# Reordering the prologue and moving attention blocks between matmuls in a fused attention and SwiGLU kernel

## The chip, the cores and the metric

The kernel runs on one core of one Trainium2 chip. The metric is the device time of one execution in microseconds (us), as the median of several executions. One execution of each kernel is also recorded by the hardware profiler; its span, from the first to the last instruction, is about 1.7 us shorter than its time. Engines: PE (tensor engine), ACT (ScalarE), DVE (VectorE), POOL (GpSimd), SP (issues transfers).

## The reference

Windowed attention (768 positions, 4 batches, 8 heads of 64, window 128, 4 sink positions) feeds an RMS-normalized SwiGLU layer:

```python
keep = is_sink | ((rel >= 0) & (rel < window))
scores = np.where(keep, q @ k.T / sqrt(64), -1e9)
x = softmax(scores) @ v                      # to (3072, 512)
xn = x / sqrt(mean(x*x) + 1e-6) * rms_g
g = xn @ w_gate                              # (512, 1536)
out = (g * sigmoid(g) * (xn @ w_val)) @ w_out
```

## The kernel before

Tokens are handled in 24 blocks of 128 (six to a batch). For every block q and k are transposed, scores, exps and masks are made, attention weights multiply v, and the rows are scaled by the RMS: `xr`. Transposing `xr` gives `xnt`, the operand of the gate and value matmuls. Four blocks form a group for the feed-forward part.

The order on PE is written by hand: a list of feed-forward "parts", and a list of attention units with the number of the part that they stand ahead of. In the prologue and in the first half of group 0 the order on DVE is by hand too, and in the prologue also that on ACT.

```python
def run(parts, slots):                # (place, unit): the unit goes ahead of that part
    slots = sorted(slots, key=lambda e: e[0])
    for s, f in enumerate(parts):
        while slots and slots[0][0] <= s:
            slots.pop(0)[1]()
        f()
    while slots:
        slots.pop(0)[1]()

with tc.manual_schedule(engines=MANUAL_ALL):          # the prologue, cut to its end
    ...
    unit_bias(1, 1)
    unit_sp(1, 1)                     # scores of block 1, then two exps on ACT
    unit_rms((0,))
    unit_rms((1,))
    unit_xr(0)                        # on ACT, behind those exps
    unit_xr(1)                        # on DVE
    unit_warm(3)                      # dummy matmuls that nothing uses
    unit_x(0)                         # transposes of xr, copy to xnt
    unit_x(1)
    ...
# group 0, first half: 14 parts, with the units of blocks 2 and 3
byhand = (fa(0, split=True) + fa(2, between=lambda: (unit_rms((2,)), unit_xr(2))) + ...)
first = fa(10) + fq(b3, 0) + fq(b3, 4) + fq(b2, 8) + fq(b3, 8)
# then `first` and the output parts of group 0 (12 parts of four 512-column matmuls),
# with the units of blocks 4 to 9 from the list FIRST (its changed lines are shown below)
```

The matmuls' results go to PSUM, for which the kernel keeps a pool of eight tiles (called banks below), given out in turn; each scores, transposes, gate, value or output tile takes one and holds it until ACT or DVE has read it.

The softmax here doesn't subtract the row's maximum and nothing guards it: scores larger than these inputs give would overflow.

## Time and profile before

| | kernel before |
|---|---|
| time, median (first 3 runs) | 251.42 us (251.39 to 251.6) |
| profiled span, mean granted PE clock | 249.9 us, 1.000 |
| PE busy | 239.6 us, 96% |
| first feed-forward matmul (L649) | 16.59 us |
| first output matmul of group 0 (L734) | 50.69 us |
| first gate matmul of group 1 | 70.69 us |
| ACT busy from 60 to 70 us | 9.4 of 10 us |

A timeline row has the start in us, the duration in us, the engine, the line of the kernel, the operation, its output and inputs, a count, and in brackets the idle time of that engine just before and what ended it. A row of the waits says who waited for whom: total us, times, longest. Since PE is the bound, I follow the three starts of the table and the end of the span: where one of them shifts, the time was lost or won ahead of it. The line of the first stands in the prediction; the other two are:

```profile
50.69 3.62 PE L734 MATMUL po<-wo,hT 128*128 128x512 bf16 x15
...
70.69 1.02 PE L649 MATMUL pg<-xnt,wg 128*128 128x512 bf16 x3
```

Two limits of this trace: it lacks 24 matmul records (1926, where e2 below, with the same matmuls, has 1950), so that some of the 10.3 us of idle time that the prediction counts is not idle: PE's waits of 0.15 us and more between its first and last matmul add up to 4.9 us, not about 6. And it holds no clock records, so its 1.000 is a default; that the clock was full there is read from its matmuls, four of which take 0.86 us.

### The profile page before, as it was taken

Reading aid. Unit: us, or ns where it says so; the run is one execution under the profiler, and the core shown is the slowest. Engines: PE = TensorE matmul, PEld = TensorE weight load, DVE = VectorE, ACT = ScalarE, POOL = GpSimd, SP = SyncE. Lnnn points to the kernel's source line nnn. Section 1 sums busy time; section 2 is a strip of 40 time slices with the busy share of each in tenths; the row PEclk is TensorE's granted clock in tenths of the full one; section 3 lists DMA queues with packets and bytes.
Section 4 is the critical chain, followed back from the end, with each engine's and each line's share of the span. In section 5 each row is a group of like instructions: output and inputs, shape, how many; then the busy total and the mean of one; then the engine's idle time right before and its main releaser. Section 6 shows DMA issues by size and latency. Waiting matters only on the chain.

```text
span 249.9 us, 5124 instructions
## 1 busy us (share of the span) xinstructions
PE 239.6 (96%) x1926; PEld 129.9 (52%) x1950; DVE 162.4 (65%) x379; ACT 142.9 (57%) x328; POOL 104.9 (42%) x141
## 2 busy tenths in 40 slices
PE   8979899999899999999999999999999999999995
PEld 3657598955454444544545444444454444444443
DVE  4857587974748779418778548769248787087800
ACT  3676657759888564874774464774374441233212
POOL 8966776497098998781330200331431000000000
DMA  9999999999939999999100465100530002610012
GB/s 128 142 185 180 190 160 206 164 153 184 133 86 134 141 158 149 138 155 154 29 3 0 91 203 107 24 3 3 132 121 0 0 3 42 169 41 3 1 64 105
DMA packets 104939, 25.51 MB, mean 102 GB/s; under 512 B 94033, under 2 KB 101969, under 8 KB 104914
## 3 DMA queue, kind: packets, MB, share of 16 engines
q0 software_dynamic: 80704, 13.90, 74.2%
q1 hardware_dynamic: 23026, 10.95, 19.7%
q10 hardware_dynamic: 1184, 0.33, 0.6%
q8 instruction: 15, 0.25, 0.4%
q14 instruction: 10, 0.08, 0.1%
HBM read 28.31 MB, written 6.29 MB: 138 GB/s over the span
## 4 chain that ended last, share of the span: by engine, by line
PE 67%; DMA 16%; POOL 8%; issue 5%; ACT 2%; DVE 1%; SPq 0%; POOLq 0%; DVEq 0%
PE po L734 20%; PE pvl L649 19%; PE pg L649 19%; DMA wv<-in_moe_w_val_dram 7%; DMA wo<-in_moe_w_out_dram 5%; DMA v<-in_v_dram 3%; PE pT L428 2%; POOL ks L108 2%; POOL v L121 2%; PE pv L475 2%; PE pv L479 2%; POOL qs L108 1%; POOL wg L140 1%; PE po L716 1%; DMA qkT<-ks 1%
## 5 line engine op out<-in xcount | busy, mean ns | idle before, releaser
L649 PE MATMUL pg<-xnt,wg 128*128 128x512 bf16 (+2 forms) x379 | 73.4, 321 | 1.3 <-ACT xnt L637 0.7
L649 PE MATMUL pvl<-xnt,wv 128*128 128x512 bf16 (+2 forms) x390 | 74.1, 322 | 0.2
L671 DVE SCALAR_TENSOR_TENSOR p<-th,pg 128x512 bf16<-128x512 bf16 x72 | 49.2, 684 | 30.4 <-ACT th L667 30.1
L667 ACT ACTIVATE th<-pg 128x512 bf16<-128x512 f32 x72 | 43.2, 602 | 41.2 <-PE pg L649 39.7
L734 PE MATMUL po<-wo,hT 128*128 128x512 bf16 x267 | 62.4, 379 | 0.5
L681 DVE TENSOR_TENSOR hT<-p,pvl 128x512 bf16<-128x512 bf16 x72 | 49.5, 687 | 8.5 <-PE pvl L649 1.5
L405 POOL TENSOR_SCALAR_AFFINE_SELECT et<-et 128x512 bf16<-128x512 bf16 x28 | 19.3, 696 | 74.4 <-ACT et L437 74.4
L649 PEld LDWEIGHTS <-wv 128*128 128x128 bf16 x392 | 33.8, 98 | 29.0
L649 PEld LDWEIGHTS <-wg 128*128 128x128 bf16 x392 | 32.7, 98 | 27.0 <-issue 1.8
L734 PEld LDWEIGHTS <-hT 128*128 128x128 bf16 x276 | 26.1, 98 | 29.2 <-issue 0.4
L437 ACT ACTIVATE et<-pT 128x512 bf16<-128x512 f32 x72 | 37.7, 613 | 3.8 <-PE pT L428 3.7
L741 ACT ACTIVATE osb<-po 128x512 f32<-128x512 f32 x23 | 13.9, 604 | 32.5 <-PE po L734 25.4
L533 ACT ACTIVATE sq<-x 128x256 bf16<-128x256 bf16 x46 | 19.4, 429 | 11.6 <-DVE x L516 11.2
L121 POOL DMA_DIRECT2D v<-in_v_dram x24 | 21.8, 909 | 4.3 <-DMA wo<-in_moe_w_out_dram 2.3
L108 POOL DMA_DIRECT2D qs<-in_q_dram x23 | 21.1, 916 | 4.6 <-DMA wo<-in_moe_w_out_dram 2.9
L511 DVE RECIPROCAL rden<-pv 128x4 f32<-128x4 f32 x48 | 7.5, 172 | 22.0 <-PE pv L479 21.9
L108 POOL DMA_DIRECT2D ks<-in_k_dram x23 | 20.9, 909 | 1.6 <-DMA wv<-in_moe_w_val_dram 0.5
L516 DVE TENSOR_TENSOR x<-pv,rden 128x256 bf16<-128x256 f32 x48 | 19.6, 422 | 0.9
L596 DVE SCALAR_TENSOR_TENSOR xr<-x,y,gb 128x512 bf16<-128x512 bf16 x22 | 16.5, 798 | 0.3
L410 POOL TENSOR_SCALAR_AFFINE_SELECT et<-et 128x512 bf16<-128x512 bf16 x22 | 14.4, 656 | 0.0
L479 PE MATMUL pv<-v,et 128*128 128x65 bf16 x160 | 12.1, 194 | 1.1 <-DVE et L403 0.9
L428 PE MATMUL pT<-qkT 64*128 64x256 bf16 (+1 forms) x160 | 11.8, 261 | 0.2 <-ACT xnt L637 0.2
(85 smaller groups left out, 194.4 us busy)
## 6 DMA issues: line engine op xcount, KB each, us to landing
out_dram<-osb SPq DMA_DIRECT2D x21, 256.0 KB, 2.4
v<-in_v_dram POOLq DMA_DIRECT2D x24, 128.0 KB, 7.1
qs<-in_q_dram POOLq DMA_DIRECT2D x23, 128.0 KB, 6.8
ks<-in_k_dram POOLq DMA_DIRECT2D x23, 128.0 KB, 6.5
wg<-in_moe_w_gate_dram POOLq DMA_DIRECT2D x6, 256.0 KB, 9.0
wv<-in_moe_w_val_dram POOLq DMA_DIRECT2D x6, 256.0 KB, 8.8
wo<-in_moe_w_out_dram POOLq DMA_DIRECT2D x2, 768.0 KB, 11.2
out_dram<-osb SPq DMA_DIRECT2D x4, 128.0 KB, 2.3
```

Of the source, the lines that this page charges most:

```text
L108: nc.gpsimd.dma_start(out=tl, in_=src[b, :, t * P:(t + 1) * P, :].rearrange("h t d -> t h d"),)
L121: nc.gpsimd.dma_start(out=V16[b][:, t, :, 0:D], in_=v[b, :, t * P:(t + 1) * P, :].rearrange("h t d -> t h d"),)
L405: nc.gpsimd.affine_select(out=ev[:, :, 0, :], in_=ev[:, :, 0, :], compare_op=ALU.is_ge, fill=0.0, base=0, pattern=[[0, x], [1, P]], channe ...
L437: nc.scalar.activation(out=et[:, hi].rearrange("p j n c -> p (j n c)"), in_=banks[u][hi], func=ACT.Exp, scale=inv_sqrt_d,)
L479: nc.tensor.matmul(out=dest, lhsT=E[(g, h, 0)], rhs=V16[b][:, t, h, :], start=(t == 0), stop=True, skip_group_check=True,)
L516: nc.vector.tensor_tensor(out=X16[g][:, heads_of(g, u), :], in0=pvv[:, :, 0:D], in1=RDEN.pop((g, u)).unsqueeze(2).to_broadcast((P, 4, D)), ...
L533: nc.scalar.activation(out=sq, in_=xh, func=ACT.Square, scale=MS_SCALE, accum_out=MS[g - i][:, i, u:u + 1],)
L649: nc.tensor.matmul(out=ps[:, i * w + c0:i * w + c0 + n], lhsT=w_sb[:, kt, ft * P:(ft + 1) * P], rhs=XNT[G][:, kt, cols], start=(kt == 0), ...
L667: nc.scalar.activation(out=st["th"], in_=st["pg"], func=ACT.Tanh, scale=0.5)
L671: nc.vector.scalar_tensor_tensor(out=p1, in0=st["th"], scalar=1.0, in1=st["pg"], op0=ALU.add, op1=ALU.mult,)
L681: LAST[0] = nc.vector.tensor_tensor(out=HT[key][:, i:i + n, cols], in0=p1.rearrange("p (n c) -> p n c", n=n), in1=st["pvl"].rearrange("p ( ...
L734: nc.tensor.matmul(out=st["po"], lhsT=HT[(G, ft // 4)][:, ft % 4, tb * P:(tb + 1) * P], rhs=wo[:, ft, :], start=(ft == 0), stop=(ft == FTN ...
```

## The change

Its intent: a shorter prologue, by putting the work that block 0 and 1 need for `xnt` into one chain, with copies and exps that are only needed later behind it; and fewer waits of PE for masks between 60 and 70 us, by putting more PE work between the steps of attention of blocks 6 to 9.

```diff
 # prologue (cut)
-        unit_bias(0, 0)
-        unit_t1(1, 0)
+        unit_t1(1, 0)
+        unit_bias(0, 0)
         unit_sp(0, 0)
+        unit_t1(1, 1)                       # k of block 1 ahead of the second bias
+        ... both other scores of blocks 0, 1, then the four attention groups ...
+        unit_t1(2, 0, held=True)            # "held": its copy is issued later
+        ...
+        while HELD:
+            HELD.pop(0)()
         unit_bias(1, 1)
-        unit_sp(1, 1)
-        unit_rms((0,))
-        unit_rms((1,))
+        unit_warm(4)
+        unit_sp(1, 1, held=True)            # its exps are issued behind xr
+        unit_rms((0, 1))                    # one group of small operations for two blocks
         unit_xr(0)                          # now on DVE
         unit_xr(1)                          # now on ACT
-        unit_warm(3)
+        unit_bias(2, 0)
+        unit_warm(2)
         unit_x(0)
+        unit_sp(2, 0, held=True)
         unit_x(1)
+        while HELD:
+            HELD.pop(0)()
 # first half of group 0
-            (3, lambda: unit_attend(2)),
-            (6, lambda: unit_t1(3, 0)),
-            (6, lambda: unit_t1(3, 1)),
-            (6, lambda: unit_x(2)),
-            (7, ...),                        # scores of 2 and 3
-            (9, lambda: unit_attend(3)),
-            (10, lambda: (unit_rms((3,)), unit_xr(3))),
+            (2, lambda: unit_attend(2)),
+            (3, lambda: (unit_rms((2,)), unit_xr(2))),
+            (5, lambda: unit_x(2)),
+            (7, lambda: unit_t1(3, 0)),
+            (8, lambda: unit_t1(3, 1)),
+            (8, ...),
+            (10, lambda: unit_attend(3)),
+            (11, lambda: (unit_rms((3,)), unit_xr(3))),
 # FIRST: attention of 6 to 9
-        (14, t(7)), (14, sink(1)), (15, s(6)), (15, t(8)), (16, x(4)), (16, x(5)),
-        (17, attend(6)), (17, s(7)), (18, t(9)), (19, attend(7)), (20, t(10)),
-        (20, sink_scores(1, 2)), (20, s(8)), (21, x(6)), (22, x(7)), (22, t(12)), (22, t(13)),
+        (16, t(7)), (16, sink(1)), (17, s(6)), (18, t(8)), (19, attend(6)), (19, s(7)),
+        (20, x(4)), (20, x(5)), (20, t(9)), (21, attend(7)), (21, sink_scores(1, 2)),
+        (21, s(8)), (22, t(10)), (22, x(6)), (24, x(7)), (24, t(12)), (24, t(13)),
```

The last list is written shorter here than in the code. Apart from these parts, four memsets move to the start, one square of block 0 goes from DVE to ACT, three more dummies are issued, and no work is removed but five small RMS operations.

More of the change, by code (lines that the diff above doesn't have):

```diff
@@ L171 @@
     nc.vector.memset(gb[0:1, 0:P], 1.0)
+    KS0 = []
+    for b in range(B):
+        KS0.append(const.tile([P, HP * KSW], BF16, name=f"ksk{b}"))
+        nc.vector.memset(KS0[b], 0.0)
     magic = const.tile([P, GB], FP32, name="magic")
@@ L256, in transposes, with unit_t1 @@
             )
-    def unit_t1(g, i):
+    HELD = []
+    def unit_t1(g, i, held=False):
         b, t = divmod(g, NT)
@@ L264, in unit_t1, with copy @@
         transposes(ps, (QS, KS_)[i].pop(g), 0)
-        (nc.scalar.copy if g in (2, 3) or g != 1 and i == 0 else nc.vector.tensor_copy)(
-            out=QKT[b][:, i, :, t * P:(t + 1) * P],
-            in_=ps[:, 0:HP * P].rearrange("p (x c) -> p x c", c=P),
-        )
+        def copy():
+            (nc.scalar.copy if g in (2, 3) or g != 1 and i == 0 else nc.vector.tensor_copy)(
+                out=QKT[b][:, i, :, t * P:(t + 1) * P],
+                in_=ps[:, 0:HP * P].rearrange("p (x c) -> p x c", c=P),
+            )
+        HELD.append(copy) if held else copy()
     def by_dma(g):
@@ L292, in unit_sink_k @@
     def unit_sink_k(b):
-        ks = sink.tile([P, HP * KSW], BF16, name="ksk")
-        nc.vector.memset(ks, 0.0)
+        ks = KS0.pop(0)
         ksv = ks.rearrange("p (h c) -> p h c", c=KSW)
@@ L365, in unit_bias, with unit_sp @@
         PTS[(g, n)] = banks
-    def unit_sp(g, n):
+    def unit_sp(g, n, held=False):
         b, t = divmod(g, NT)
@@ L379, in unit_sp, with exps @@
                 )
-        for hi in range(2):
-            et = epool.tile([P, HP, P], BF16, name="etp", bufs=6)
-            nc.scalar.activation(
-                out=et.rearrange("p x c -> p (x c)"), in_=banks[hi],
-                func=ACT.Exp, scale=inv_sqrt_d,
-            )
-            for hp in range(HP):
-                E[(g, 2 * hp + hi, n)] = et[:, hp, :]
+        def exps():
+            for hi in range(2):
+                et = epool.tile([P, HP, P], BF16, name="etp", bufs=6)
+                nc.scalar.activation(
+                    out=et.rearrange("p x c -> p (x c)"), in_=banks[hi],
+                    func=ACT.Exp, scale=inv_sqrt_d,
+                )
+                for hp in range(HP):
+                    E[(g, 2 * hp + hi, n)] = et[:, hp, :]
+        HELD.append(exps) if held else exps()
     def bank(name="pT"):
@@ L526, in unit_sq @@
         sq = xpool.tile([P, 4, D], BF16, name="sq")
-        if g == 0:
+        if (g, u) == (0, 1):
             nc.vector.scalar_tensor_tensor(
@@ L539 @@
     GROUP = {}
-    for gs in [(0,), (1,), (2,), (3,), (4, 5), (6,), (7,)] + [
+    for gs in [(0, 1), (2,), (3,), (4, 5), (6,), (7,)] + [
             tuple(range(g, g + GB)) for g in range(2 * GB, NB, GB)]:
@@ L588, in unit_xr @@
         xr = xpool.tile([P, DM], BF16, name="xr", bufs=4)
-        if g == 0:
+        if g == 1:
             nc.scalar.mul(xr, x16, y)
-        elif g == 1:
+        elif g == 0:
             nc.vector.tensor_scalar(
@@ L784, in unit_attend01 @@
         unit_norm(g, u, PV[(g, u)])
-        unit_sq(g, u)
     with tc.manual_schedule(engines=MANUAL_ALL):
@@ L792 @@
         unit_t1(0, 1)
+        unit_t1(1, 0)
         unit_bias(0, 0)
-        unit_t1(1, 0)
         unit_sp(0, 0)
+        unit_t1(1, 1)
+        unit_bias(0, 1)
+        unit_sp(0, 1)
+        unit_bias(1, 0)
+        unit_sp(1, 0)
         unit_sink_k(0)
-        unit_bias(0, 1)
-        unit_t1(1, 1)
-        unit_sp(0, 1)
         unit_attend01(0, 0)
-        unit_bias(1, 0)
         unit_attend01(0, 1)
-        unit_sp(1, 0)
+        unit_sq(0, 0)
         unit_gt()
         unit_attend01(1, 0)
-        unit_t1(2, 0)
+        unit_sq(1, 0)
+        unit_t1(2, 0, held=True)
         unit_attend01(1, 1)
-        unit_t1(2, 1)
+        unit_sq(1, 1)
+        unit_sq(0, 1)
+        unit_t1(2, 1, held=True)
+        while HELD:
+            HELD.pop(0)()
         unit_bias(1, 1)
-        unit_sp(1, 1)
-        unit_rms((0,))
-        unit_rms((1,))
+        unit_warm(4)
+        unit_sp(1, 1, held=True)
+        unit_rms((0, 1))
         unit_xr(0)
         unit_xr(1)
-        unit_warm(3)
+        unit_bias(2, 0)
+        unit_warm(2)
         unit_x(0)
+        unit_sp(2, 0, held=True)
         unit_x(1)
-        unit_bias(2, 0)
-        unit_sp(2, 0)
+        while HELD:
+            HELD.pop(0)()
     h0 = slice(0, GN // 2)
@@ L828, in fq @@
         return parts_f(0, tuple(range(ft, ft + 4)), cols)
-    byhand = (fa(0, split=True) + fa(2, between=lambda: (unit_rms((2,)), unit_xr(2)))
-              + fa(4) + fq(b2, 0) + fa(6) + fq(b2, 4) + fa(8))
+    byhand = (fa(0, split=True) + fa(2) + fa(4) + fq(b2, 0) + fa(6) + fq(b2, 4) + fa(8))
     first = fa(10) + fq(b3, 0) + fq(b3, 4) + fq(b2, 8) + fq(b3, 8)
@@ L837 @@
             (2, lambda: unit_gb()),
-            (3, lambda: unit_attend(2)),
-            (6, lambda: unit_t1(3, 0)),
-            (6, lambda: unit_t1(3, 1)),
-            (6, lambda: unit_x(2)),
-            (7, lambda: unit_sink_scores(0, 3, 1)),
-            (7, lambda: unit_bias(2, 1)),
-            (7, lambda: unit_sp(2, 1)),
-            (7, lambda: unit_bias(3, 0)),
-            (7, lambda: unit_sp(3, 0)),
-            (9, lambda: unit_attend(3)),
-            (10, lambda: (unit_rms((3,)), unit_xr(3))),
+            (2, lambda: unit_attend(2)),
[3 more added lines that the diff above has]
+            (8, lambda: unit_t1(3, 1)),
+            (8, lambda: unit_sink_scores(0, 3, 1)),
+            (8, lambda: unit_bias(2, 1)),
+            (8, lambda: unit_sp(2, 1)),
+            (8, lambda: unit_bias(3, 0)),
+            (8, lambda: unit_sp(3, 0)),
+            (10, lambda: unit_attend(3)),
+            (11, lambda: (unit_rms((3,)), unit_xr(3))),
         ])
@@ L863 @@
         (10, lambda: unit_attend(5)),
-        (14, lambda: unit_t(7)),
-        (14, lambda: unit_sink(1)),
-        (15, lambda: unit_s(6)),
-        (15, lambda: unit_t(8)),
-        (16, lambda: unit_x(4)),
-        (16, lambda: unit_x(5)),
-        (17, lambda: unit_attend(6)),
-        (17, lambda: unit_s(7)),
-        (18, lambda: unit_t(9)),
-        (19, lambda: unit_attend(7)),
-        (20, lambda: unit_t(10)),
-        (20, lambda: unit_sink_scores(1, 2)),
-        (20, lambda: unit_s(8)),
-        (21, lambda: unit_x(6)),
-        (22, lambda: unit_x(7)),
-        (22, lambda: unit_t(12)),
-        (22, lambda: unit_t(13)),
+        (16, lambda: unit_t(7)),
+        (16, lambda: unit_sink(1)),
+        (17, lambda: unit_s(6)),
+        (18, lambda: unit_t(8)),
+        (19, lambda: unit_attend(6)),
+        (19, lambda: unit_s(7)),
+        (20, lambda: unit_x(4)),
+        (20, lambda: unit_x(5)),
+        (20, lambda: unit_t(9)),
+        (21, lambda: unit_attend(7)),
+        (21, lambda: unit_sink_scores(1, 2)),
+        (21, lambda: unit_s(8)),
+        (22, lambda: unit_t(10)),
+        (22, lambda: unit_x(6)),
+        (24, lambda: unit_x(7)),
+        (24, lambda: unit_t(12)),
+        (24, lambda: unit_t(13)),
     ]
```

## The prediction

> **What bounds the kernel now.** I read the page's busy shares first, then the waits of the tensor engine (PE), then the timeline of the first 36 us engine by engine, then that of 50 to 80 us.
>
> ```profile
> span 249.9 us, 5124 instructions
> PE 239.6 (96%) x1926; PEld 129.9 (52%) x1950; DVE 162.4 (65%) x379; ACT 142.9 (57%) x328; POOL 104.9 (42%) x141
> ```
>
> PE is the bound: 10.3 us of the span are idle. Some 2.9 us of those are the tail after the last matmul and 1.06 us are the start, so about 6 us in the middle can be won at the very most, 2.5%. The waits of PE name them:
>
> ```profile
> PE pxt L623 <- ACT xr L590: 1.3, 1, 1.3
> PE pv L479 <- DVE et L403: 0.9, 2, 0.5
> PE pg L649 <- ACT xnt L637: 0.7, 1, 0.7
> PE pT L374 <- ACT qkT L265: 0.6, 1, 0.6
> PE pxt L623 <- DVE xr L596: 0.5, 1, 0.5
> PE pv L461 <- DVE p L671: 0.3, 1, 0.3
> PE pv L479 <- POOL et L405: 0.2, 1, 0.2
> ```
>
> Busy time also holds the dummy matmuls (L348), so the quantity to follow is when the first feed-forward matmul (L649) starts, and how late PE is afterwards. The timeline of the end of the prologue:
>
> ```profile
> 13.51 1.09 ACT L382 ACTIVATE etp<-pT 128x512 bf16<-128x512 f32 x2
> 14.28 0.43 DVE L592 TENSOR_SCALAR xr<-x,y 128x512 bf16<-128x512 bf16 x1
> 14.48 0.74 ACT L590 ACTIVATE xr<-x,y 128x512 bf16<-128x512 bf16 x1
> 15.27 0.62 PE L623 MATMUL pxt<-ident,xr 128*128 128x128 bf16 x8 [1.32 <-ACT xr L590]
> 15.70 1.29 DVE L630 TENSOR_TENSOR xnt<-pxt,gt 128x512 bf16<-128x512 bf16 x2 [0.99 <-PE pxt L623]
> 16.59 0.62 PE L649 MATMUL pg<-xnt,wg 128*128 128x128 bf16 x8
> ```
>
> The reader sees PE waiting for the scaled x of block 0, which sits on ScalarE (ACT) behind two exps that nobody needs yet. From 54.8 to 73 us it is ACT that paces everything; its timeline there has one idle stretch over 0.2 us:
>
> ```profile
> 54.78 1.01 ACT L287 COPY qkT<-pqk 128x1024 bf16<-128x1024 bf16 x1 [0.68 <-PE pqk L253]
> ...
> 65.47 0.42 ACT L533 ACTIVATE sq<-x 128x256 bf16<-128x256 bf16 x1 [0.63 <-DVE x L516]
> ...
> 73.02 0.69 ACT L667 ACTIVATE th<-pg 128x512 bf16<-128x512 f32 x1
> ```
>
> **What the Trainium skill says.** "TensorE: Matmul & The Clock Gate", section Part 1 (architectural detail), says that ScalarE and VectorE (DVE) take their work in strict queue order. The trace agrees: the xr above, whose input was done at 13.25, started at 14.48 when the exps were through. The same page, section "Wait — 56ns, not 53.3ns?", gives 215.7 ns between starts of warm 512-column matmuls and 426.7 ns of cold ones. Here four output matmuls take 0.86 us (216 ns each), and the first nine dummies take 4.02 us, so dummies are slow only at the start. "Perfetto Trace Analysis", section "Per-instruction lifecycle", says that a PE record's end is a model; so I count PE by starts.
>
> **The change, part by part.**
>
> *Prologue.* Order on each engine is fixed, so I push times through it with durations of this trace.
> - Up to the first scores (PE 7.00) and the third and fourth exp nothing moves: the bias pair, the k transposes and the scores are the same work in another order. Block 1's second use of k comes earlier, so the scores that feed exps 5 and 6 no longer stand behind two attention groups. The six exps, 7.43 to 10.83 with two small gaps now, end about 10.55: 0.25 us earlier.
> - Both attention groups of block 0 and the 1.05 us of gain matmuls (L179) then stand before block 1's attention, which starts about 10.8 instead of 10.62. DVE does reciprocal (0.21) and product (0.34 to 0.46) twice; squares on ACT end about 13.05; rms is now one group of 7 small operations for both blocks instead of two of 6. The only seven-operation group in this trace (two columns, from 53.65) took 1.24, two groups of 6 here took 12.19 to 14.25, 2.06. So y is ready about 14.3, as now.
> - The gain: xr of block 1 (0.74 on ACT) starts at 14.3 with no exp ahead, and block 0, which is needed first, gets the DVE form (0.43): ready about 14.74. Its transposes start 14.78 instead of 15.27; the copy on DVE is then ready about 15.95. In the kernel before, transposes of both blocks and then bias and scores of block 2 (0.86 us) stood between; now the bias is done in the wait. First L649 at about 15.95 instead of 16.59: **-0.65 us**. The second dummies (6 instead of 3) and the four memsets (0.1 each, before a 0.74 us DVE wait) lie in waits.
>
> *Block 2 and 3.* Attention of 2 moves ahead of the second gate matmuls, and x(2) ahead of the third value part. From attention start to x(2): average product +1.3, square; but one tanh now stands between the two squares on ACT, so rms starts at +2.86 (now +2.49); rms 1.10 and xr 0.75 bring x(2) to +4.7. PE has 0.71 + 3 x 0.87 = 3.3 us of work for it. A stall of 1.4 us, where now there are 0.46 + 0.67 = 1.13; against that, the transposes of block 3 (0.45), which filled this gap, come later in a place that is free. Net **-0.15**. Attention of 3 comes one part (0.87) later while x(3) stays: xr at +4.72, PE there at +0.71 + 4 x 0.885 = +4.25. A stall of **+0.5** that the kernel before lacks (its x(3) at 36.31 waited for nothing). So 0.3 us of lead are left.
>
> *Attention of 6 to 9.* The transposes of block 7 go two output parts later (2 x 0.86 = 1.73 us). PE loses its mask waits of 0.33 and 0.53 in their old places. But ACT, in strict order, must do from there to the copy that the scores of block 9 need: an output copy 0.49, copies of blocks 7 to 10 at 0.9 each, exps of 6, 7, 8 at 4 x 0.49 each, sink copies and exp 0.85, squares of 6 and 7 at 0.8 each, two x copies 1.0, another output copy 0.49: 14.2 us. It can begin when the second output block is through, 50.69 - 0.26 + 6 x 0.8625 + 0.24 = 55.85, so it ends at 70.1 if it never waits. Then scores of 9 and attention of 8 (0.55 + 0.71) come before the next gate matmul: 71.4, where now it is 70.69. With the lead that is a loss of 1.0 in this stage, 1.7 if ACT waits 0.7 us for masks and parts; the sink scores of 8 also stand behind block 9's copy now. I take **+0.9**, a bit under, because the later exps then overlap better and slots of this kind had been chosen by someone for a reason that I may not see. Tanh of the next stage is less far behind PE, which should take away the 0.33 wait at 79.43: **-0.2**.
>
> Sum: -0.65 - 0.15 + 0.5 + 0.9 - 0.2 = +0.4 us, 251.8.
>
> **The rivals.** (a) Prologue gain carried to the end, the spreading hides the mask waits (0.33 + 0.53 + 0.25 + 0.21): -0.7 - 1.2, 249.6. For it: those waits are in the trace and the spreading is aimed at them. Against: ACT's count above. (b) ACT is the full bound from 56 to 72: +1.7 there, 252.6. For it: hardly an idle moment in its timeline; against: it idles 0.6 us once and the later exps may be shorter of waits. (c) The weights arrive too late for an earlier start, the gain is hidden. Against: GpSimd's next issues waited for earlier weight transfers, and those waits place the first w_v chunk at about 14.8 and the second at 18.9, both before their use. (d) Block 1's k, asked for about 0.2 us earlier, isn't there yet: it would cost 0.2 at most.
>
> **Range and chances.** The parts are uncertain by about 0.3 (prologue), 0.5 (blocks 2, 3), and 0.9 (6 to 9); together about 1.1 us, so 250.3 to 253.2. For over 2% the change would have to move 5 us, almost all idle time that PE has, or to add as much to it: 0.02 and 0.02.
>
> **What would show it.** Right: first L649 of the changed kernel about 15.95, its xr wait shorter than 0.6; a PE wait of over 1 us before x(2), about 0.5 before x(3); ACT without a gap from about 56 to 71, a PE wait for qkT (L297) before scores of 9, and the first 512-column gate matmul about 0.7 later than 70.69. Wrong: that gate matmul before 70.2, or no ACT-copy wait of PE between 60 and 72; a wait for a weight or k transfer in the first 20 us; or a change of over 0.5 us in the stages after 80 us, which I take to move as a whole.

## The result

The changed kernel took 254.44 us (median of 4 runs: 254.63, 254.49, 254.38, 252.77) against 251.51 us (251.39 to 251.6) of the kernel before. A ratio is the mean time of one kernel's fast runs over that of the other's of the same rounds, so it isn't quite the ratio of the medians; here it is 1.0102, with a 95% interval of 1.0059 to 1.0145. That is slower, but by less than 2%; the time lies above the predicted range.

The four runs are of two kinds. Three had a mean granted clock of 0.992 or 0.993; the fourth, 1.7 us faster, had 1.000.

The page of the changed kernel, PE clock in 40 slices of 6.3 us, in tenths of full speed:

```profile
PEclk9999999999979999999999999999999999999999
```

The twelfth slice, 69.5 to 75.9 us, has 7. (The page of the kernel before has no such row, as its trace holds no clock records.) The waits of PE in the changed kernel:

```profile
PE pxt L636 <- DVE xr L609: 2.6, 3, 1.2
PE pT L441 <- ACT qkT L297: 1.3, 1, 1.3
...
PE pss L342 <- ACT qkT L297: 0.8, 1, 0.8
PE pv L492 <- DVE et L416: 0.7, 2, 0.4
```

The waits for `xr` grew from 1.8 us (1.3 and 0.5 above) to 2.6, although that of the prologue is gone. Two waits for `qkT` copies on ACT, 2.1 us together, are new. The mask waits, at which the spread was aimed, are 0.7 us instead of 0.9 on DVE, and the one of 0.2 on POOL is gone.

The timeline of the changed kernel, end of the prologue:

```profile
4.86 0.62 ACT L199 CAST qs<-osb 128x512 bf16<-128x512 f32 x1 [2.25 <-DMA osb<-in_q_dram]
...
14.41 0.72 ACT L603 ACTIVATE xr<-x,y 128x512 bf16<-128x512 bf16 x1 [0.32 <-DVE y L591]
...
14.95 0.40 PE L636 MATMUL pxt<-ident,xr 128*128 128x128 bf16 x4
...
16.12 0.61 PE L662 MATMUL pg<-xnt,wg 128*128 128x128 bf16 x8
```

`xr` now waits for `y` (0.32 us) and not for exps, and PE reaches the transposes without a wait. The first feed-forward matmul starts at 16.12, 0.47 earlier, though q's cast began 0.26 later in this execution (4.86; 4.60 in the profiled one of before). How early that transfer lands differs between executions of both kernels.

The timeline of PE in the changed kernel, where it waits for `xr` of blocks 2 and 3:

```profile
24.21 0.40 PE L636 MATMUL pxt<-ident,xr 128*128 128x128 bf16 x4 [1.24 <-DVE xr L609]
36.77 0.40 PE L636 MATMUL pxt<-ident,xr 128*128 128x128 bf16 x4 [0.93 <-DVE xr L609]
```

And of DVE in front of the second of them:

```profile
32.17 0.69 DVE L694 TENSOR_TENSOR hT<-p,pvl 128x512 bf16<-128x512 bf16 x1
32.77 0.17 DVE L524 RECIPROCAL rden<-pv 128x4 f32<-128x4 f32 x1
```

In the kernel before, it started as soon as the attention matmuls were through:

```profile
31.86 0.18 DVE L511 RECIPROCAL rden<-pv 128x4 f32<-128x4 f32 x1 [0.75 <-PE pv L479]
```

Block 3's reciprocal now stands behind a product of the feed-forward part on DVE. The first output matmul comes at 51.20 instead of 50.69: the lead of 0.47 has become a lag of 0.51.

```profile
51.20 5.34 PE L747 MATMUL po<-wo,hT 128*128 128x512 bf16 x24
```

The timeline of ACT at the ends of the later stage in the changed kernel:

```profile
56.58 0.60 ACT L754 ACTIVATE osb<-po 128x512 f32<-128x512 f32 x1 [1.97 <-PE po L747]
57.07 1.01 ACT L297 COPY qkT<-pqk 128x1024 bf16<-128x1024 bf16 x1
...
70.39 1.05 ACT L297 COPY qkT<-pqk 128x1024 bf16<-128x1024 bf16 x1
```

Then PE's:

```profile
71.49 0.61 PE L441 MATMUL pT<-qkT 64*128 64x256 bf16 x8 [1.32 <-ACT qkT L297]
...
72.87 1.90 PE L662 MATMUL pg<-xnt,wg 128*128 128x512 bf16 x4
74.56 1.63 PE L662 MATMUL pvl<-xnt,wv 128*128 128x512 bf16 x4
```

ACT stood idle for 1.97 us ahead of the stage, began block 7's copy 2.3 us later than before (57.07 against 54.78), and from there was busy with 0.16 us of pause until block 10's copy ended, for which PE waited. Four gate matmuls then take 1.69 us from start to start (72.87 to 74.56) instead of 0.86: half the clock. By stretches (per engine busy us and count, the mean granted clock, the transfer share, GB/s):

```profile
70.00:71.00 1.00, 0.17 (x4) 0.09 (x1) 0.42 (x1) 1.00 (x3) 1.00 (x3) 1.00 0.00 0
71.00:72.00 1.00, 0.51 (x10) 0.44 (x9) 0.00 (x0) 1.00 (x3) 0.97 (x2) 1.00 0.61 221
72.00:74.00 2.00, 2.00 (x23) 1.17 (x20) 1.12 (x4) 2.00 (x5) 0.94 (x2) 0.59 0.58 123
74.00:76.00 2.00, 2.00 (x6) 0.70 (x5) 0.40 (x1) 1.47 (x7) 2.00 (x4) 0.56 0.48 94
76.00:78.00 2.00, 2.00 (x14) 1.02 (x13) 1.25 (x3) 0.78 (x2) 2.00 (x3) 1.00 0.74 91
```

PE, the first number after the stretch's length, was hardly used from 70 to 72 us, and from 72.4 to 75.8 its clock was at 0.50. The clock is back at 1.00 as abruptly as it went.

So the trace gives a first account of the 3.0 us between the two profiled spans: -0.47 at the start of the feed-forward part, +0.98 up to the first output matmul, +1.67 up to the first gate matmul of group 1 (72.87 against 70.69, a lag of 2.18, the last 0.2 of it already at half clock), +1.4 more for the half clock, and -0.6 later. The experiments test it.

### The profile page after: what moved, and what is told of

Same layout as the page of the kernel before. It is cut to its first block, busy times and chain, and to the rows that moved or that the text cites. A ratio compares the mean times of both kernels' runs of the same rounds, so it can differ in the third digit from the quotient of the medians.

```text
span 252.9 us, 5149 instructions
## 1 busy us (share of the span) xinstructions
PE 241.9 (96%) x1953; PEld 130.4 (52%) x1953; DVE 160.9 (64%) x372; ACT 143.0 (57%) x330; POOL 105.3 (42%) x141
## 4 chain that ended last, share of the span: by engine, by line
PE 85%; ACT 6%; DVE 5%; DMA 2%; issue 1%; ACTq 0%; DVEq 0%
PE pg L662 24%; PE pvl L662 23%; PE po L747 22%; PE pT L441 3%; PE pv L488 2%; PE pv L492 2%; DMA osb<-in_k_dram 2%; ACT et L450 2%; PE pqk L257 1%; ACT sq L546 1%; PE pT L368 1%; PE po L729 1%; PE pT L383 1%; DVE xr L609 1%; DVE x L529 1%
## 5 line engine op out<-in xcount | busy, mean ns | idle before, releaser
L662 PE MATMUL pg<-xnt,wg 128*128 128x512 bf16 (+2 forms) x392 | 75.2, 325 | 0.1
L662 PE MATMUL pvl<-xnt,wv 128*128 128x512 bf16 (+2 forms) x392 | 74.9, 324 | 0.0
L423 POOL TENSOR_SCALAR_AFFINE_SELECT et<-et 128x512 bf16<-128x512 bf16 x22 | 14.3, 652 | 0.0
## 6 DMA issues: line engine op xcount, KB each, us to landing
wo<-in_moe_w_out_dram POOLq DMA_DIRECT2D x2, 768.0 KB, 11.9
```

The costliest lines, as they stand in the source:

```text
L662: nc.tensor.matmul(out=ps[:, i * w + c0:i * w + c0 + n], lhsT=w_sb[:, kt, ft * P:(ft + 1) * P], rhs=XNT[G][:, kt, cols], start=(kt == 0), ...
```

## The experiments

**Theory 1**: new prologue good (about -0.65), x(3) costs, the spread costs because ACT's queue starts later, and PE's idling there lets the clock fall. **Theory 2**: the loss comes from blocks 2 and 3, and the later stage only carries it. **Rival on the clock**: its fall is chance, or due to the load after the gap.

All kernels gave correct results. "Before" is the kernel before on the same chip in the same rounds; its medians were 251.6, 251.6 and 251.56 in the three groups of runs (three chips), so I also compare runs of different groups. Three of its 37 runs took 252.86 to 253.17; the record gives these three a mean clock of 0.992, and 0.998 or 1.000 to the others for which it lists one.

| label | prologue | blocks 2, 3 | blocks 6 to 9 | median (range), us | ratio to before, 95% |
|---|---|---|---|---|---|
| e1_spread_undone | new | new | as before | 251.98 (251.95 to 252.25) | 1.0006 (0.9985 to 1.0028) |
| e2_spread_alone | as before | as before | spread | 253.24 (252.2 to 255.51) | 1.0062 (1.0021 to 1.0103) |
| e3_prologue_alone | new | as before | as before | 250.90 (250.87 to 251.08) | 0.9962 (0.9939 to 0.9985) |
| e4_warm_in_gap | new | new | spread, 4 dummies | 252.81 (252.77 to 252.97) | 1.0038 (1.0017 to 1.0059) |
| e5_middle_undone | new | as before | spread | 253.50 (251.77 to 253.54) | 1.0051 (1.0027 to 1.0076) |
| e6_earlier_by_one | new | as before | one part earlier | 250.14 (250.06 to 250.27) | 0.9940 (0.9927 to 0.9953) |
| e7_later_by_one | new | as before | one part later | 251.30 (251.17 to 251.7) | 0.9987 (0.9975 to 0.9999) |
| e8_middle_new | new | reworked | as before | 249.62 (249.47 to 250.19) | 0.9922 (0.9910 to 0.9934) |
| e9_x3_back | new | new, but attention of 3 as before | as before | 250.86 (250.82 to 251.03) | 0.9968 (0.9946 to 0.9989) |
| e10_no_new_dummies | new, no new dummies | as before | as before | 250.95 (250.91 to 252.37) | 0.9982 (0.9957 to 1.0007) |
| e11_best_one | new | reworked | one part earlier | 249.33 (248.96 to 251.03) | 0.9915 (0.9884 to 0.9946) |
| e12_best_two | new | reworked | two parts earlier | 248.83 (248.62 to 248.94) | 0.9885 (0.9861 to 0.9909) |

### e1: undo the spread

```diff
 # FIRST of the changed kernel
-        (16, lambda: unit_t(7)), ... (24, lambda: unit_t(13)),
+        (14, lambda: unit_t(7)), ... (22, lambda: unit_t(13)),     # all as before
```

> The changed kernel with only the places of attention 6 to 9 as they were before (new prologue and new places of blocks 2 and 3 kept). Theory 1 (the spread costs 1.7 us of ScalarE order and, through the tensor engine idling, the half clock of about 1.7 us more): both go, only the late start of x(3) remains (+0.46 at the gate matmul behind it), so 251.9 (251.6 to 252.2), clock 1.000 in all runs, no wait for qkT before the scores of block 9. Theory 2 (the loss comes from the new places of blocks 2 and 3, the later stages only carry it): still over 253, clock below 1 in most runs.

251.98 us, all six runs within 0.3 us, clock 1.000. No wait for `qkT` is left in the stage; the waits before x(2) (1.24) and x(3) (0.94) are as in the changed kernel. Theory 2 falls: most of the loss sat in the spread. The new places of blocks 2 and 3 can account for the remaining 0.4 us over before; e9 tests that.

### e2: the spread alone

```diff
 # FIRST of the kernel before
-        (14, lambda: unit_t(7)), ... (22, lambda: unit_t(13)),
+        (16, lambda: unit_t(7)), ... (24, lambda: unit_t(13)),
```

> The kernel before with only the places of attention 6 to 9 as changed. Theory 1: first 512-column gate matmul 1.5 to 1.9 us later than 70.69, a wait of over 1 us for qkT before the scores of block 9, 253.0 in runs with full clock and about 254.6 in runs whose clock falls to half for some 3 us after 72 us. Theory 2: 251.5 to 251.8, clock 1.000.

The six runs fall into three kinds: 252.2 to 252.47 (three), 254.02 and 254.12, and 255.51. The wait for `qkT` before block 9's scores is 1.31 us. The profiled run is the slowest one, with a mean clock of 0.987: its clock fell twice, after the spread's gap and already in the old prologue. The second shows in its stretches:

```profile
14.00:15.00 1.00, 0.00 (x0) 0.00 (x0) 0.69 (x2) 1.00 (x2) 1.00 (x2) 1.00 1.59 203
15.00:16.00 1.00, 0.85 (x9) 0.86 (x10) 0.28 (x1) 0.09 (x1) 1.00 (x2) 0.63 1.42 188
16.00:17.00 1.00, 1.00 (x8) 0.16 (x7) 1.00 (x2) 0.00 (x0) 0.28 (x2) 0.50 1.46 196
```

The 1.32 us wait for `xr` that the prediction found in the kernel before is thus also a place where the clock can fall. The full-clock runs are 0.6 to 0.9 us over before, less than the 1.5 that I expected, and 0.6 us come back behind the stage (see e4).

### e3: the prologue alone

```diff
 # the changed kernel, with `byhand` and FIRST of the kernel before
```

> The changed prologue with the places of all later attention as before. If the prologue gives the 0.65 us of the prediction and nothing takes it back: 250.9 (250.6 to 251.1), first L649-kind matmul at about 15.9 if q lands at 4.60. If a later wait (x(2), masks) takes the gain back: 251.3 to 251.6.

250.90 us, a gain of 0.70 us on the median of before. The first feed-forward matmul starts at 15.94 with q's cast at 4.67. The gain survives to the end: the first gate matmul of group 1 comes at 69.95 instead of 70.69. All six runs are within 0.21 us.

### e4: keep PE busy in the gap

```diff
         (24, lambda: unit_t(13)),
+        (24, lambda: unit_warm(4)),       # four dummy matmuls ahead of the scores of block 9
```

> The changed kernel with four dummy matmuls (0.86 us at full clock) in the 1.3 us wait before the scores of block 9; they compute nothing that is used. Theory 1, clock part (the clock falls because the tensor engine was idle in a large part of 66 to 72 us): the clock stays at 1.000 in all or nearly all runs, time 252.8 where the changed kernel shows 252.8 or 254.4. Rival (the fall is chance, or follows from the load after the gap): still half or more of the runs at 254.4 with clock 0.993.

252.81 us, all six runs within 0.2 us, where the changed kernel had 254.4 in three of four. The stretches of this kernel:

```profile
70.00:71.00 1.00, 1.00 (x8) 0.34 (x6) 0.42 (x1) 1.00 (x3) 1.00 (x3) 1.00 0.00 0
71.00:72.00 1.00, 0.55 (x11) 0.52 (x10) 0.00 (x0) 1.00 (x3) 1.00 (x2) 1.00 0.59 217
72.00:74.00 2.00, 2.00 (x28) 1.13 (x24) 1.12 (x4) 2.00 (x5) 0.93 (x2) 1.00 0.58 123
```

The same scores start at 71.51 (71.49 in the changed kernel), so the dummies delay nothing, and the clock stays at 1.00. The rival on the clock falls: the load behind the gap is the same, and without dummies the spread had a fallen clock in 10 of 16 runs (changed kernel, e2, e5), with them in none of six. In which executions it falls stays a matter of chance. In the 3.4 us from 68.9 to 72.3, PE was busy 1.60 us (47%) in the changed kernel, and 2.47 us (73%) here.

Since its clock is whole, e4 against e1 is the cost of the spread by itself: 0.83 us (252.81 - 251.98). At the first gate matmul of group 1 it is 1.52 (72.66 against 71.14); 0.63 comes back between 80.1 and 81.5 us, where e1, like the kernel before, makes PE's attention of block 9 wait for DVE's product. The attention tile takes no data from the product; that it waits for the PSUM bank which the product still reads is inferred from the code and not tested. The waits of both give it 0.33 us, counted from a modelled end; from start to start the second of the two matmuls comes 0.60 us late (lines at e6).

### e5: only blocks 2 and 3 as before

```diff
 # the changed kernel, with `byhand` and its list of places from the kernel before
```

> New prologue and spread, with the places of blocks 2 and 3 as before. If the parts add (prologue alone gave 250.9, the spread at full clock 0.83 between two earlier runs): 251.75 at full clock, 253.4 in runs whose clock falls after 72 us; no wait before x(3). If the middle part were what makes the spread hurt (rival: both stages share one cause, a late x(3)), it would be at 250.9 to 251.1, without a clock fall.

Two runs at 251.77 and 251.88, four at 253.5 with a mean clock of 0.993. Both numbers are as the sum of the parts says; the clock falls without any part of the middle changed. The wait for `qkT` is again 1.32 us.

### e6 and e7: one part earlier, one part later

```diff
 # e3, every place from 14 on in FIRST
-        (14, lambda: unit_t(7)), ...
+        (13, lambda: unit_t(7)), ...      # e6
+        (15, lambda: unit_t(7)), ...      # e7
```

> New prologue, middle as before, and attention 6 to 9 one output part (0.86 us) EARLIER than before. ScalarE theory (this stage is paced by ScalarE's queue, which is idle for 0.7 us before the copy of block 7): the mask waits shrink and the time falls by 0.2 to 0.8 below 250.9, to about 250.4. Rival (the mask waits follow from the distance in tensor work alone, which the shift leaves as it is): 250.8 to 251.0.

> As the run before, but one part LATER than the kernel before (the change moved them by about two). ScalarE theory: half-way, 251.1 to 251.5 at full clock, with a wait for qkT before scores of 8 or 9 that the kernel before lacks. If only the order within the spread (t(10) behind the exps of 8) hurts and not the delay: 250.8 to 251.0.

With e3 as the middle, the row is: one part earlier 250.14, as before 250.90, one later 251.30, spread by about two 251.8 at full clock (e5). The starts on PE show that these times mix two effects:

| places of blocks 6 to 9 | first output matmul to first gate matmul of group 1 | from there to the first output matmul of group 1 |
|---|---|---|
| one part earlier (e6) | 19.74 us | 24.91 us |
| as before (e3) | 19.99 us | 25.53 us |
| one part later (e7) | 20.87 us | 24.91 us |
| spread, full clock (e4, with the new middle) | 21.44 us | 24.91 us |

In the stage itself later is worse in every step, as the ACT theory says. But earlier won only 0.25 us there. The other 0.62 us of e6 is the bank wait behind the stage, which each of these three shifts removes, the later ones too; why the old places have it was not tested. In e3 and in e6 the two matmuls are:

```profile
78.11 0.27 PE L474 MATMUL pv<-vsk,esk 64*128 64x260 bf16 x1
78.70 0.27 PE L474 MATMUL pv<-vsk,esk 64*128 64x260 bf16 x1 [0.33 <-DVE p L684]
...
78.00 0.28 PE L474 MATMUL pv<-vsk,esk 64*128 64x260 bf16 x2
```

So e6's time fell into my range partly by luck: its mask waits on DVE even grew, from 0.8 to 1.2 us, and with the bank wait it would have been near the rival's 250.8. In e7 the wait for `qkT` that I expected does not appear among PE's; it has mask waits on DVE of 1.1 us and waits for `xr` of 0.8 us (e3: 0.8 and 0.4).

### e8: another middle

```diff
 # e3
-    byhand = (fa(0, split=True) + fa(2, between=lambda: (unit_rms((2,)), unit_xr(2))) + ...
+    byhand = (fa(0, split=True) + fa(2) + ...
-            (3, lambda: unit_attend(2)),
-            (6, lambda: unit_t1(3, 0)),
-            (6, lambda: unit_t1(3, 1)),
+            (2, lambda: unit_attend(2)),
+            (3, lambda: (unit_rms((2,)), unit_xr(2))),
+            (5, lambda: unit_t1(3, 0)),
+            (5, lambda: unit_t1(3, 1)),
             (6, lambda: unit_x(2)),
-            (7, lambda: unit_sink_scores(0, 3, 1)),
-            (7, lambda: unit_bias(2, 1)),
-            (7, lambda: unit_sp(2, 1)),
+            (6, lambda: unit_sink_scores(0, 3, 1)),
+            (6, lambda: unit_bias(2, 1)),
+            (6, lambda: unit_sp(2, 1)),
```

> New prologue, attention 6 to 9 as before, and in the middle: attention of 2 early as in the change, transposes of 3 ahead of x(2), scores of block 2's second half behind x(2), attention of 3 as before. It is to take away the 0.41 wait before x(2) and most of the 0.67 behind it, without the wait at x(3): 249.9 to 250.4. If x(2) still waits because its chain of squares and rms is longer with the tanh between: 250.6 to 251.

249.62 us, better than I expected by 0.3. The transposes of `xr` of block 2, in PE's timeline, have no wait ahead of them any more:

```profile
24.20 0.40 PE L636 MATMUL pxt<-ident,xr 128*128 128x128 bf16 x4
```

and there is no wait for `xnt` behind them either, because scores fill the time of the copy.

### e9: only x(3) back

```diff
 # e1
-            (10, lambda: unit_attend(3)),
-            (11, lambda: (unit_rms((3,)), unit_xr(3))),
+            (9, lambda: unit_attend(3)),
+            (10, lambda: (unit_rms((3,)), unit_xr(3))),
```

> The run with the spread undone (251.98), but attention of 3, its rms and xr one place earlier, where they stood before; attention of 2 and x(2) stay as changed. It tells which of the two middle moves costs. If x(3) alone (its 0.93 us wait and the products that precede the reciprocals): the wait before x(3) goes and 250.9 (250.7 to 251.1), equal to the prologue alone. If the x(2) wait of 1.24 us costs too: 251.2 to 251.6.

250.86 us, as the prologue alone. So of the middle's two moves that of block 3's attention cost 1.12 us (251.98 - 250.86), and that of block 2, with the transposes and scores of block 3 behind it, cost nothing (250.86 against 250.90), although its wait of 1.2 us is still in the profile: it stands in the place of other waits and of the transposes of block 3.

### e10: without the new dummies

```diff
 # e3
-        unit_warm(4)
-        unit_warm(2)
```

> The prologue-alone kernel without the six dummy matmuls behind the two last attention groups; all else equal. Clock theory (an idle stretch of the tensor engine at 12 to 15 us lets the clock fall to half from about 15 us in some runs, as seen in one run of the spread alone): 250.7 to 250.9 in runs with full clock, 252.2 to 252.9 in the others, and at least one of six of those. Rival (dummies have no effect on the clock there): all six at 250.7 to 251.0, clock as with dummies.

Inconclusive, though it leans to the clock theory: five runs at 250.91 to 251.43 and one at 252.37. The record gives that one a mean clock of 0.993 and the others 0.998 to 1.000, so its clock did fall, as the theory asks; it was not profiled, so the place isn't shown, and one of six against none of six in e3 can be chance (e11, which has the dummies, also had one such run). From 11.9 to 15.3 us PE was busy 1.96 us (58%) here, 3.10 us (91%) in the changed kernel, and 1.46 us (43%) in the kernel before.

### e11 and e12: what the runs point to

```diff
 # e8, every place from 14 on in FIRST
-        (14, lambda: unit_t(7)), ...
+        (13, lambda: unit_t(7)), ...      # e11
+        (12, lambda: unit_t(7)), ...      # e12
```

> New prologue, reworked middle (249.62 alone), attention 6 to 9 one part earlier (0.76 alone). If the two gains add: 248.9 (248.6 to 249.2). If the earlier tensor work only meets the same ScalarE queue: 249.4 to 249.7.

> As the run before, but attention 6 to 9 two parts earlier than in the kernel before. If ScalarE's earlier start still pays: 248.4 to 248.8. If its queue is full by then or attention of 5 and output copies collide with it: 248.9 to 249.5.

e12 beats both kernels: 248.83 us in four runs within 0.32 us, 2.7 us less than before and between its two expected ranges. e11 scattered between 248.96 and 249.61, with one run at 251.03, whose mean clock the record gives as 0.992. The gains of e6 and e8 add only in part there: its profiled run (249.61) still has the bank wait behind the stage (0.44 us from start to start), which e12's profile lacks.

## Why the prediction was wrong

Taken by its own steps, with what measured each alone:

| step | predicted | measured | by |
|---|---|---|---|
| prologue | -0.65 | -0.70 | e3 against before |
| attention and x of block 2 | -0.15 | -0.04 | e9 against e3 |
| x of block 3 | +0.5 | +1.12 | e1 against e9 |
| attention of 6 to 9, with the later -0.2 | +0.7 | +0.83 | e4 against e1 |
| sum at full clock | +0.4 | +1.2 | e4 against before: 252.81 - 251.6 |
| clock at half for 3.4 us | none | +1.7, in 3 of 4 runs | changed kernel's runs: 254.4 against 252.77 |

**The step that failed** is the one on the clock. The prediction put it: "so dummies are slow only at the start". It used the skill's page for the length of matmuls at either clock, and did not ask whether the new waits, which it had itself worked out, would bring the slow clock back. With full clock the changed kernel took 252.77, inside the range of 250.3 to 253.2 and close to its rival (b), 252.6; that closeness is luck, since the spread cost less than (b) says (0.83 instead of 1.7 - 0.2) and x(3) more (1.12 instead of 0.5). The range had no room for the 1.7 us that come at once with the clock, and e4, which only adds four dummies, takes them away.

**The mis-sized term** is x(3). The mechanism was right: attention of 3 was one part later, its squares parted by a tanh, x(3) where it was. What I left out is on DVE: by moving behind the value matmuls, block 3's reciprocal also came behind their product and its multiply, so it began 1.34 us after the start of the attention matmuls (31.43 to 32.77) instead of 0.66 (31.20 to 31.86 in the kernel before). The "+4.72" for `xr` was moreover block 2's chain: for block 3 the trace before the change already showed +5.00 (31.20 to 36.20), and the changed kernel took +5.28 (31.43 to 36.71). The wait is 0.93 instead of 0.5. That the reciprocal, and not the tanh, makes the difference is read from this timeline; no run moved it alone. The second term of that kind, the spread, was as good as right in its sum, but only because two parts err against each other: 1.52 us at the gate matmul where I took 0.9, and 0.63 given back where I took 0.2. I had counted 1.0 to 1.7 there, and shaded it down with a reason that no row of the profile gave. The count had a slip too: its terms add up to 13.9 us, not 14.2; ACT took 14.9 (56.58 to 71.44).

**What held**: the prologue's path (y at about 14.3: 14.18 in e3, and 14.38 in the changed kernel's profile, where q came 0.26 us late; the first feed-forward matmul at 15.95: 15.94 in e3); the wait of over 1 us before x(2) (1.24); ACT without a gap from 56 to 71 us (56.58 to 71.44 with 0.16 of pause); the wait for `qkT` before scores of block 9. Rival (a), that the spread hides the waits of the stage, is right on 0.6 of the 1.3 us that it lists (0.24 and 0.45 are left, on masks), but the stage as a whole lost 1.52. Rival (c), late weights, shows in no run. Rival (d), k of block 1 not there yet, shows as a wait of 0.3 us in e5's profile and in no other of PE's waits that I read, so it is an event of single executions.

**What stays open**: where the clock fell in the kernel before's three runs at 253 (by the record it did, to a mean of 0.992; none was profiled, but e2's profile shows the fall with the same prologue); why it is so rare there, with a stretch as idle as the spread's; why the old places have the bank wait; and why e11 scatters.

## What to carry to other kernels

When an engine is the bound and a second one paces a stretch of it, moving the second's work later to hide its waits moves the whole queue behind it: look for idle time ahead of the stretch on the pacing engine (here ACT's, 0.68 us in the kernel before and 1.97 in the changed one) and try to start its work earlier: in this stage one part earlier won 0.25 us and one part later lost 0.88. Then look behind the stage before you credit the move: 0.62 us more went with a wait for a PSUM bank there, whichever way the work moved. When you move a unit, push it through every engine's queue, as a reciprocal that slipped behind two products helped to cost 1.12 us here. And add up PE's busy share over a few microseconds wherever a change adds waits: here the clock fell behind stretches of 43 and 47%, which cost 1.7 us in the changed kernel; four dummy matmuls in a wait that existed anyway delayed nothing and kept it up.

## What the Trainium skill lacked or had wrong

- "TensorE: Matmul & The Clock Gate", section "What's actually happening", has the clock fall after at least one idle window of about 3.4 us, and its section "HAM oscillation — how this bites in real kernels" gives as the rule no PE-idle gaps over about 3.4 us. That is too weak: here it fell with no single wait over 1.32 us. In the traces of the changed kernel, e2 and e5 every change of the clock lies a whole number of 3.41 us behind the first clock record. PE was busy 47, 43, 47 and 47% of the 3.41 us ahead of the four falls in mid-kernel (e2 has two); among all such windows of the traces with clock records, the lowest share that no fall followed is 60% (e3, 244.2 to 247.7 us). The page's section "A second HAM failure mode: psum-queue depth-cycling" does tell of short, frequent idle times that make the clock swing, but gives no such share. The slow spell lasted one window, 72.4 to 75.8 us.
- That page tells of run-to-run chance only for the start of a kernel. Here falls came in mid-kernel, in some executions and not in others (10 of 16 with the spread), so that one kernel's times fall into two kinds (252.77 and about 254.5 us).
